# x of groups 4 and 5 transposed by DMA instead of by TensorE, between two sets of loads

## The chip, the cores and the metric

One core of one Trainium2 chip. The metric is the device time of one execution in microseconds (us). "Before" is the kernel as it was, "changed" the kernel with the change. A ratio is the mean time of one kernel's fast runs over that of the other's of the same rounds, so it is not quite the ratio of the medians quoted beside it.

## The reference

Attention within chunks of 64 tokens, then a feed-forward layer with a squared ReLU:

```python
scores = (1 / sqrt(64)) * q_c @ k_c^T          # chunks of 64 tokens, 8 x 8 heads, 576 tokens each
attn   = softmax(scores)
x      = (attn @ v_c)  rearranged to [4608, 512]
out    = (relu(x @ w_in) ** 2) @ w_out         # w_in 512 x 2048, w_out 2048 x 512
```

## The kernel before

The 4608 tokens are 18 groups of 256; two groups make a block of 512, for which the feed-forward layer runs (`ffn_in`, L360, then `ffn_out`, L412). While a block's matmuls run, the attention of the next block is slipped in between them: `plan` names for each slot (a few matmuls) what is issued there. A slot is a place in each engine's order, not a time. `TA` transposes q and k on TensorE; `C` and `TD` cast them on GpSimd and transpose them by DMA, from group 6 on; `SC` are the scores, `AV` the values, which leave x in SBUF; `XT` transposes x, as the feed-forward layer wants it with the features on the partitions.

```python
    FIRST_DMA_T = 6
    FIRST_DMA_X = 6
    # ... cut ...
    def transpose_x(g):
        # ... cut: xT tile of the block ...
        x = state.pop(("x", g))
        dst = xTs[j][:, c // 128:c // 128 + 2].rearrange("p t h q -> p (t h) q")
        if g >= FIRST_DMA_X:
            nc.sync.dma_start_transpose(out=dst, in_=x.rearrange("p t h a d -> p (t h a d)"))
            return
        ps = ps_att.tile([128, 1024], FP32, name="ps_att")
        psb = ps.bitcast(BF16)[:, 0:1024].rearrange("p (b q) -> p b q", q=128)
        for t in range(2):
            for hp in range(n_hp):
                nc.tensor.transpose(                                   # L342, 8 a group
                    out=psb[:, t * n_hp + hp, :],
                    in_=x[:, t, hp].rearrange("p a d -> p (a d)"), identity=ident)
        copy = nc.scalar.copy if g == 3 else nc.vector.tensor_copy
        copy(out=dst, in_=psb)                                         # L347
    # ... cut ...
        elif j == 1:       # block 1 (groups 2, 3): nxt = groups 4, 5; far = groups 6, 7
            loads = itertools.chain(*map(qk_pieces, far), v_pieces(far[0]))
            go_slots = range(14, 32)
            # ... cut ...
            for i, g in enumerate(nxt):
                for slot, f in ((21 + 4 * i, TA), (28 + 2 * i, SC), (33 + 2 * i, AV),
                                (38 + 3 * i, XT)):
                    at(slot, f, g)
            for i, g in enumerate(far):
                at(34 + 3 * i, C, g)
                at(36 + 3 * i, TD, g)
```

All loads and all DMA transposes are issued from SyncE, in order; output stores are issued from GpSimd (but for the last two).

The softmax here doesn't subtract the row's maximum and nothing guards it: scores larger than these inputs give would overflow.

## Time and profile before

| | us |
|---|---|
| median of the four executions beside the changed kernel | 294.42 |
| span in the profile | 292.4 |
| TensorE busy | 285.6 (98%) |

The prediction below shows what bounds the kernel; here are the rows that the change acts on, from the groups of instructions by line (last: busy us, mean ns of one, idle time before) and from the DMA issues (last: us from issue to landing).

```profile
L342 PE MATMUL ps_att<-ident,x 128*128 128x128 bf16 x32 | 2.6, 219 | 0.0
L347 DVE COPY xT<-ps_att 128x1024 bf16<-128x1024 bf16 x3 | 2.1, 692 | 4.4 <-PE ps_att L342 4.4
qkT<-qkb SPq DMA_TRANSPOSE x12, 5.8
xT<-x SPq DMA_TRANSPOSE x12, 3.3
```

32 transposes of L342 are those of groups 2 to 5, eight each. The 12 transposes of xT by DMA are those of groups 6 to 17. A busy time of 2.6 us for 32 instructions of 219 ns says that they overlap.

### The profile page before, as it was taken

Reading aid. Unit: us, or ns where it says so; the run is one execution under the profiler, and the core shown is the slowest. Engines: PE = TensorE matmul, PEld = TensorE weight load, DVE = VectorE, ACT = ScalarE, POOL = GpSimd, SP = SyncE. Lnnn points to the kernel's source line nnn. Section 1 sums busy time; section 2 is a strip of 40 time slices with the busy share of each in tenths; the row PEclk is TensorE's granted clock in tenths of the full one; section 3 lists DMA queues with packets and bytes.
Section 4 is the critical chain, followed back from the end, with each engine's and each line's share of the span. In section 5 each row is a group of like instructions: output and inputs, shape, how many; then the busy total and the mean of one; then the engine's idle time right before and its main releaser. Section 6 shows DMA issues by size and latency. Waiting matters only on the chain.

```text
span 292.4 us, 6471 instructions
## 1 busy us (share of the span) xinstructions
PE 285.6 (98%) x2661; PEld 141.7 (48%) x2661; DVE 111.0 (38%) x234; ACT 131.2 (45%) x214; POOL 66.8 (23%) x107
## 2 busy tenths in 40 slices
PE   7899999999999999999999999999999999999995
PEld 3454445885544444444444444444444444444444
DVE  0458413665414710571068105710472046104401
ACT  1557315775137513761376137612761276127410
POOL 2047824001510241042122113311043100230010
PEclk9999999999999999999999999999999999999999
DMA  7999999978999999999998899188999911331011
GB/s 233 248 349 366 352 294 255 345 160 192 214 165 209 211 213 206 250 198 232 263 232 170 189 231 214 37 184 211 201 209 224 202 39 36 74 72 36 0 74 72
DMA packets 145933, 56.00 MB, mean 191 GB/s; under 512 B 127024, under 2 KB 141616, under 8 KB 145904
## 3 DMA queue, kind: packets, MB, share of 16 engines
q1 hardware_dynamic: 142896, 46.28, 75.1%
q0 software_dynamic: 2864, 9.18, 10.2%
q8 instruction: 21, 0.34, 0.5%
q10 hardware_dynamic: 144, 0.13, 0.1%
q14 instruction: 8, 0.07, 0.1%
HBM read 36.70 MB, written 9.44 MB: 158 GB/s over the span
## 4 chain that ended last, share of the span: by engine, by line
PE 83%; DMA 8%; SPq 4%; POOL 2%; issue 0%; DVE 0%; DVEq 0%
PE ps_ffn L360 39%; PE ps_ffn L412 37%; DMA w_st<-in_moe_w_out_dram 4%; DMA w_st<-in_moe_w_in_dram 4%; PE ps_att L315 2%; SPq L138 2%; PE ps_att L291 2%; SPq L150 2%; PE ps_ffn L401 1%; PE ps_ffn L431 1%; PE ps_att L196 1%; POOL w_out_bf L179 1%; POOL w_in_bf L172 1%; PE ps_att L342 1%; POOL w_in_bf L168 1%
## 5 line engine op out<-in xcount | busy, mean ns | idle before, releaser
L360 PE MATMUL ps_ffn<-xT,w_in_bf 128*128 128x512 bf16 (+3 forms) x648 | 130.0, 356 | 0.2 <-POOL w_in_bf L168 0.2
L372 DVE TENSOR_TENSOR gT<-rl 128x512 bf16<-128x512 bf16 x144 | 71.2, 510 | 135.7 <-ACT rl L370 134.7
L412 PE MATMUL ps_ffn<-w_out_bf,gT 128*128 128x512 bf16 x496 | 109.3, 379 | 0.0
L370 ACT ACTIVATE rl<-ps_ffn 128x512 bf16<-128x512 f32 x144 | 85.1, 599 | 37.3 <-PE ps_ffn L360 35.8
L360 PEld LDWEIGHTS <-w_in_bf 128*128 128x128 bf16 x648 | 61.3, 98 | 60.4 <-POOL w_in_bf L168 0.9
L412 PEld LDWEIGHTS <-gT 128*128 128x128 bf16 x496 | 47.8, 98 | 56.3
L419 ACT COPY o_sb<-ps_ffn 128x512 f32<-128x512 f32 x31 | 18.2, 586 | 93.0 <-PE ps_ffn L412 93.0
L389 POOL DMA_DIRECT2D out_dram<-o_sb x39 | 21.2, 545 | 119.1 <-ACT o_sb L419 115.8
L270 POOL CAST qkb<-qk_sb 128x1024 bf16<-128x1024 f32 x24 | 25.8, 1085 | 76.2 <-DMA qk_sb<-in_q_dram 72.5
L323 DVE TENSOR_TENSOR x<-ps_att,rec 128x512 bf16<-128x512 f32 x36 | 24.9, 691 | 1.2
L298 ACT ACTIVATE e<-ps_att 128x1024 bf16<-128x1024 f32 x18 | 17.7, 1023 | 2.3 <-PE ps_att L291 2.3
L431 PE MATMUL ps_ffn<-w_out_bf,gT 128*128 128x512 bf16 x64 | 15.0, 379 | 0.3 <-POOL w_out_bf L179 0.3
L264 PE MATMUL ps_ffn<-zeros 128*128 128x512 bf16 x29 | 9.5, 466 | 1.3 <-POOL zeros L57 1.3
L179 POOL CAST w_out_bf<-w_st 128x1024 bf16<-128x1024 f32 x8 | 9.1, 1131 | 6.9 <-DMA w_st<-in_moe_w_out_dram 6.8
L315 PEld LDWEIGHTS <-e 64*64 64x64 bf16 x576 | 6.6, 107 | 7.5 <-DVE gT L372 2.1
L322 DVE RECIPROCAL rec<-ps_att 128x8 f32<-128x8 f32 x36 | 7.2, 199 | 7.1 <-PE ps_att L315 7.0
L431 PEld LDWEIGHTS <-gT 128*128 128x128 bf16 x64 | 6.0, 98 | 7.4 <-issue 0.6
L315 PE MATMUL ps_att<-ve_sb,e 64*64 64x65 bf16 x288 | 8.8, 196 | 0.1
L315 PE MATMUL ps_att<-vo_sb,e 64*64 64x65 bf16 x288 | 8.8, 196 | 0.0
L205 ACT COPY qkT<-ps_att 128x512 bf16<-128x512 bf16 x8 | 4.3, 589 | 9.7 <-PE ps_att L196 9.7
L172 POOL CAST w_in_bf<-w_st 128x1024 bf16<-128x1024 f32 x7 | 7.4, 1062 | 2.9 <-DMA w_st<-in_moe_w_in_dram 2.9
L291 PEld LDWEIGHTS <-qkT 64*64 64x64 bf16 x576 | 5.7, 108 | 4.7 <-issue 3.4
(33 smaller groups left out, 59.8 us busy)
## 6 DMA issues: line engine op xcount, KB each, us to landing
out_dram<-o_sb POOLq DMA_DIRECT2D x31, 256.0 KB, 4.0
qk_sb<-in_q_dram SPq DMA_DIRECT2D x20, 256.0 KB, 5.3
qk_sb<-in_k_dram SPq DMA_DIRECT2D x20, 256.0 KB, 5.4
ve_sb<-in_v_dram SPq DMA_DIRECT2D x32, 128.0 KB, 4.1
w_st<-in_moe_w_in_dram SPq DMA_DIRECT2D x8, 512.0 KB, 6.7
w_st<-in_moe_w_out_dram SPq DMA_DIRECT2D x8, 512.0 KB, 6.1
vo_sb<-in_v_dram SPq DMA_DIRECT2D x24, 128.0 KB, 3.6
qk_sb<-in_q_dram SPq DMA_DIRECT2D x4, 512.0 KB, 7.0
```

The source lines that it names most:

```text
L179: nc.gpsimd.tensor_copy(out=w_out_bf[:, 2 * i:2 * i + 2, :], in_=st)
L270: nc.gpsimd.tensor_copy(out=qkb[:, which], in_=qk[g][which].rearrange("p t h d -> p (t h d)"))
L298: nc.scalar.activation(out=e.rearrange("p a h t q -> p (a h t q)"), in_=ps, func=AF.Exp, scale=scale)
L315: nc.tensor.matmul(out=ps[64 * p:64 * p + 64, a, hp * (D + 1):(hp + 1) * (D + 1)], lhsT=e[64 * c:64 * c + 64, a, hp, t, :], rhs=vb[64 * c: ...
L323: nc.vector.tensor_tensor(out=x[:, t].rearrange("p h a d -> p a h d"), in0=o[:, :, :, 0:D], in1=rec.to_broadcast([128, 2, n_hp, D]), op=AL ...
L360: nc.tensor.matmul(out=h[:, o:o + n], lhsT=w_in_bf[:, dt, ft * 128:(ft + 1) * 128], rhs=xT[:, c // 128:(c + n) // 128, dt, :], start=(dt = ...
L370: nc.scalar.activation(out=rl, in_=h, func=AF.Relu)
L372: nc.vector.tensor_tensor(out=gTs[j][:, ft:ft + per, c:c + 512 // per], in0=r3, in1=r3, op=ALU.mult)
L389: eng.dma_start(out=out[b * S + s:b * S + s + m, cols], in_=o_sb[p:p + m, :])
L412: nc.tensor.matmul(out=o_ps, lhsT=gT[:, ft, tt * 128:(tt + 1) * 128], rhs=w_out_bf[:, ft, :], start=(ft == 0), stop=(ft == n_ft - 1))
L419: nc.scalar.copy(out=o_sb, in_=o_ps)
L431: nc.tensor.matmul(out=o_ps[tt], lhsT=gT[:, ft, tt * 128:(tt + 1) * 128], rhs=w_out_bf[:, ft, :], start=(ft == 0), stop=(ft == n_ft - 1))
```

## The change

Groups 4 and 5 go by DMA too. For that their `XT` moves up in the order, and the value loads of group 6 and the q,k transposes of groups 6 and 7 move behind it. As built, the change removes 16 transposes and their 16 weight loads from TensorE and two copies from VectorE, and puts two DMA transposes into SyncE's order, ahead of the value loads of group 6. Nothing else moves on any engine.

```diff
-    FIRST_DMA_X = 6
+    FIRST_DMA_X = 4
@@ block 1
-            go_slots = range(14, 32)
+            go_slots = [*range(14, 22), *range(39, 44)]
-                                (38 + 3 * i, XT)):
+                                (36 + 2 * i, XT)):
-                at(36 + 3 * i, TD, g)
+                at(44 + 2 * i, TD, g)
```

## The prediction

> **What bounds the kernel now.** I read the page first: busy time per engine, the slices, and the chain that ended last.
>
> ```profile
> PE 285.6 (98%) x2661; PEld 141.7 (48%) x2661; DVE 111.0 (38%) x234; ACT 131.2 (45%) x214; POOL 66.8 (23%) x107
> PE   7899999999999999999999999999999999999995
> PEclk9999999999999999999999999999999999999999
> DMA  7999999978999999999998899188999911331011
> PE 83%; DMA 8%; SPq 4%; POOL 2%; issue 0%; DVE 0%; DVEq 0%
> ```
>
> TensorE is busy in every slice at its full granted clock, and 83% of the chain is TensorE. The DMA engines are nearly full from slice 10 (73 us) to slice 20. Then I took the chain in order of time, because the mean share does not tell which wait ends last in the stage that changes:
>
> ```profile
> 72.96 0.39 PE ps_att L315 x32
> 73.35 2.70 PE ps_ffn L412 x12
> 76.04 0.45 PE ps_att L342 x8
> 76.49 2.59 PE ps_ffn L412 x12
> 79.08 0.45 PE ps_att L342 x8
> 79.53 5.18 PE ps_ffn L412 x24
> 84.71 7.77 PE ps_ffn L360 x36
> ...
> 95.55 0.38 PE ps_att L291 x32
> ```
>
> From 44.9 us to 289 us this chain is TensorE without a gap. So here a TensorE instruction removed is time removed, unless some input comes later than TensorE then wants it. The two pieces of L342 (eight transposes each, x of groups 4 and 5) are what the change takes away. L360 at 84.71 is the first user of their result, L291 at 95.55 the scores of group 7.
>
> **What the Trainium skill says.** (1) "Perfetto Trace Analysis", Identifying the Most-Contended Engine: busy share of matmuls is no good measure of the distance to the limit. The trace agrees (98% beside 48% of weight loads), so I cost the change from the chain, not from the 98%. (2) "TensorE: Matmul & The Clock Gate", Part 4: PE-mode transpose: a 128x128 bf16 transpose measured some 390 ns alone and 275 ns in a kernel, and its output in PSUM needs a copy. Here one shows 219 ns, but eight together hold the chain only 0.45 us, because they are pipelined; I use 0.45. (3) "DMA: Bandwidth & Descriptors", Issuing engines are not separate DMA queues: transfers share 16 engines whoever starts them. The trace agrees, as the landing times below show. (4) Same page, Latency and other measured facts: transposing DMA at 261 GB/s in one kernel. This trace has a duration: late in the kernel, one x transpose has the engines to itself.
>
> ```profile
> 246.00:248.00 2.00, 2.00 (x41) 0.94 (x40) 1.25 (x4) 1.19 (x2) 0.00 (x0) 1.00 0.49 95
> 248.00:250.00 2.00, 2.00 (x11) 0.94 (x10) 1.72 (x5) 0.00 (x0) 0.00 (x0) 1.00 0.19 36
> ```
>
> The last two columns are DMA share and GB/s: 2 x 0.49 + 2 x 0.19 = 1.36 us of all 16 engines for 262 KB, 193 GB/s, slower than that figure. The measurement decides.
>
> **The change part by part.**
>
> Removed from TensorE: 16 transposes, two pieces of 0.45 us, all on the chain: **-0.90 us**. Nothing else moves on TensorE: in the order of its instructions as built, the 32 rows (16 weight loads, 16 transposes) are the only difference.
>
> Removed from VectorE: two copies from PSUM of 0.69 us. VectorE is 38% busy, and none of its work stands in this stretch of the chain: 0 us.
>
> Added to the DMA: two transposes of x. The built order of the SyncE queue shows them as the only addition, ahead of the five value loads of group 6. The new slots of the qkT transposes (44 and 46) and of the loads change no order beyond that. When do they start? The queue now:
>
> ```profile
> 71.61 2.39 SPq L131 DMA_DIRECT2D qk_sb<-in_q_dram  x1
> 74.05 0.78 SPq L131 DMA_DIRECT2D qk_sb<-in_k_dram  x1
> 74.87 1.64 SPq L138 DMA_DIRECT2D ve_sb<-in_v_dram  x2
> 76.56 2.00 SPq L150 DMA_DIRECT2D vo_sb<-in_v_dram  x3
> 78.74 7.62 SPq L277 DMA_TRANSPOSE qkT<-qkb  x2
> 86.40 1.22 SPq L138 DMA_DIRECT2D ve_sb<-in_v_dram  x2
> ```
>
> The x transposes take the place at 74.87. The last multiplication that makes x of group 4 ends at 72.84 and that of group 5 at 75.06 (timeline of VectorE), so SyncE hardly waits. One issue took 1.26 us (median of the 12 there are): 74.9 and 76.1. The value loads issued at those times landed in 4.5 and 4.0 us, transposes of x in 3.0 to 5.4, so xT is there by about 81.5; L360 wants it at 84.7 - 0.9 = 83.8. **Hidden, with some 2 us to spare.**
>
> What it pushes: everything after on the queue starts about 2 x 1.26 = 2.5 us later, and the engines get 2 x 1.36 = 2.7 us more work. The shares in two-us windows are 0.63 at 74 to 76, then 1.07 to 1.53 up to 86 (packets overlap, so more than 1 is possible), so little of it fits in a hole: at most 2 x (1 - 0.63) = 0.7 us. Estimate of the push: **2.0 to 2.7 us**. Who feels it? Landing now, the time when TensorE now uses it, and what is left after 0.9 us earlier use and 2.7 us later landing (the worst of my estimate):
>
> - qkT of group 7: issued 81.9, landing 10.3 us later, 92.2; scores at 95.5: 3.3 left now, **-0.3** after (+0.4 with a push of 2.0).
> - qkT of group 6: issued 78.7, +8.2, 86.9; scores at 92.4: 5.5 now, 1.9 after.
> - values of group 7: last issued 88.6, +5.7, 94.3; used at 101.0: 6.7 now, 3.1 after.
> - xT of group 7: issued 105.4, +4.3, 109.7; used at 114.5: 4.8 now, 1.2 after.
> - qkT of group 9: issued 111.5, +7.5, 119.0; used at 123.4: 4.4 now, 0.8 after.
>
> So one deadline is about met or just missed. That row's landing view (the window holds this transpose alone):
>
> ```profile
> L277 SPq DMA_TRANSPOSE qkT<-qkb x1: 4457/4457/4457, 81.9 to 81.9; - x1
> DMA to landing us min/median/max: 10.3/10.3/10.3
> ```
>
> Those 10.3 us are queueing: the least that such a transpose took in this trace is 4.5. Two output stores, issued at 82.2 and 85.6, lie on the same engines and take 8.9 and 6.3 us.
>
> Sum: -0.90 us on the chain, plus a wait of 0 to about 1 us before the scores of group 7. I put it at +0.25 us on average (four chances in ten of about 0.6 us): 294.34 - 0.90 + 0.25 = 293.7.
>
> **Rivals.** *A. The whole gain arrives (293.4).* For it: every other transfer has slack, and qkT of group 7 now meets less of the stores, which come 0.4 to 0.9 us earlier while it comes later. Against: its slack is gone by arithmetic. *B. A new wait takes the gain back (294.0 to 296).* The pushed qkT of group 7 comes 0.5 to 2.5 us late, or, if the push isn't absorbed, qkT of group 9 too. For it: DMA shares above 1 and landings of 8 to 10 us between 79 and 92. Against: an early wait gives the DMA queue time and loosens the later deadlines, so the waits don't add up without end; SyncE stands idle from 180 to 187.7 anyway, so nothing lasts beyond. *C. xT itself late.* It would stop L360 at 83.8 at once. For it: the first transpose follows eight loads of 262 KB. Against: 2 us of slack, and the loads there land in 4 to 4.5 us. *D. The transposes were hidden anyway (294.3).* It would need something other than TensorE to end the waits at 76 and 79; the chain shows no gap there, so I give it little.
>
> **Range and chances.** The centre is 293.6, between A's 293.4 and the sum 293.7. Low end: 293.4 less the scatter of the three runs (0.3) is about 292.9. High end: B with two waits of about 0.8 us, 293.4 + 1.6, about 295.1. 2% is 5.9 us: more than six times all that the removed work costs, and for slower it would take a push more than twice that of my estimate at several deadlines. So within 2% is nearly certain.
>
> **What would show each step.** L342 with 16 transposes instead of 32 and two transposes more by DMA of xT; no L342 between 73 and 84 in the chain, and L360 starting at about 83.8 (right) or later with a wait for the DMA of xT (C). Landing of qkT of group 7 near 94.5, and the weight load of its scores near 94.6: a wait on that DMA there is B, none is A. The last TensorE work starting 0.9 us earlier than now is A. I am wrong if the time goes outside the range: if the push is well over 2.7 us because mixed transposes and stores slow each other more than now, or if a wait shows at three or more of the five deadlines.

## The result, and the profile after

| | before | changed |
|---|---|---|
| median, us | 294.42 (294.0 to 294.53) | 293.34 (293.18 to 294.32) |
| ratio of fast runs | | 0.9973 (95%: 0.9949 to 0.9997) |
| span in the profile | 292.4 | 291.6 |

The same rows of the changed kernel:

```profile
L342 PE MATMUL ps_att<-ident,x 128*128 128x128 bf16 x16 | 1.4, 220 | 0.0
L347 DVE COPY xT<-ps_att 128x1024 bf16<-128x1024 bf16 x1 | 0.7, 691 | 0.6 <-PE ps_att L342 0.6
xT<-x SPq DMA_TRANSPOSE x14, 3.9
qkT<-qkb SPq DMA_TRANSPOSE x12, 6.9
```

Half of L342 is gone, and two of the copies of L347. The chain in order of time (start us, us, what), in the stage that changed:

```profile
73.10 0.39 PE ps_att L315 x30
73.49 0.16 issue
73.65 10.31 PE ps_ffn L412 x47
83.96 7.77 PE ps_ffn L360 x36
91.73 0.38 PE ps_att L291 x32
```

Where two pieces of 0.45 us stood in the chain before, there is one run of L412 now, and L360 follows it without a wait for the DMA. (47 where it should be 48: some matmul records are missing from a trace.)

One measure serves for the rest of this text: **the stretch**, from the first weight load of the scores of group 5 to that of the scores of group 6. It holds both XT. These are the weight loads, before and after (start us, us, what; in brackets the idle time of the weight loads before it):

```profile
68.01 0.33 PEld L291 LDWEIGHTS <-qkT 64*64 64x64 bf16 x32 [0.21 <-issue]
92.41 0.34 PEld L291 LDWEIGHTS <-qkT 64*64 64x64 bf16 x32 [0.42 <-issue]
...
68.16 0.33 PEld L291 LDWEIGHTS <-qkT 64*64 64x64 bf16 x32 [0.21 <-issue]
91.66 0.33 PEld L291 LDWEIGHTS <-qkT 64*64 64x64 bf16 x32 [0.42 <-issue]
94.73 0.34 PEld L291 LDWEIGHTS <-qkT 64*64 64x64 bf16 x32 [0.42 <-issue]
```

The stretch was 68.01 to 92.41 = 24.40 us before, and is 68.16 to 91.66 = 23.50 us now: 0.90 us less. It doesn't feel what happens before 68 us, where executions differ by some tenths.

Now the SyncE queue of the changed kernel (start us, us, what):

```profile
70.67 3.03 SPq L131 DMA_DIRECT2D qk_sb<-in_k_dram  x1
74.22 3.37 SPq L336 DMA_TRANSPOSE xT<-x  x2
77.64 1.14 SPq L138 DMA_DIRECT2D ve_sb<-in_v_dram  x2
78.83 1.97 SPq L150 DMA_DIRECT2D vo_sb<-in_v_dram  x3
80.98 9.27 SPq L277 DMA_TRANSPOSE qkT<-qkb  x2
90.29 1.13 SPq L138 DMA_DIRECT2D ve_sb<-in_v_dram  x2
```

The pair of x is issued from 74.22, the second at 75.7, and lands 3.9 us later, at 79.7: four us ahead of L360. The qkT transposes start 2.2 us later than before (80.98 against 78.74), the value loads behind them 3.9 us later (90.29 against 86.40). That was to make qkT of group 7 late. Its landing view, for this one transpose:

```profile
L277 SPq DMA_TRANSPOSE qkT<-qkb x1: 6076/6076/6076, 84.2 to 84.2; - x1
DMA to landing us min/median/max: 9.5/9.5/9.5
```

It landed at 93.7, the weight load of its scores came at 94.73: one us to spare. No wait. Nor was any of the prediction's other four deadlines missed: qkT of group 6 landed at 91.0 for a weight load at 91.7, the values of group 7 at 95.5 for 100.2, x of group 7 at 111.3 for 113.4, qkT of group 9 at 120.6 for 122.5.

### The profile page after: what moved, and what is told of

The parts are those of the page before. It is cut to its first block, busy times and chain, and to the rows that moved or that the text cites. A ratio compares the mean times of both kernels' runs of the same rounds, so it can differ in the third digit from the quotient of the medians.

```text
span 291.6 us, 6425 instructions
## 1 busy us (share of the span) xinstructions
PE 282.5 (97%) x2624; PEld 140.5 (48%) x2645; DVE 109.1 (37%) x232; ACT 131.2 (45%) x214; POOL 66.3 (23%) x107
## 4 chain that ended last, share of the span: by engine, by line
PE 81%; DMA 8%; SPq 4%; POOL 2%; DVE 1%; ACT 1%; issue 1%; DVEq 0%
PE ps_ffn L360 37%; PE ps_ffn L412 37%; DMA w_st<-in_moe_w_out_dram 4%; DMA w_st<-in_moe_w_in_dram 4%; SPq L138 2%; PE ps_att L315 2%; SPq L150 2%; PE ps_att L291 2%; PE ps_ffn L401 1%; PE ps_ffn L431 1%; PE ps_att L196 1%; POOL w_out_bf L179 1%; POOL w_in_bf L172 1%; ACT rl L370 1%; POOL w_in_bf L168 1%
## 5 line engine op out<-in xcount | busy, mean ns | idle before, releaser
L360 PE MATMUL ps_ffn<-xT,w_in_bf 128*128 128x512 bf16 (+3 forms) x648 | 130.0, 356 | 0.0
L412 PE MATMUL ps_ffn<-w_out_bf,gT 128*128 128x512 bf16 x481 | 107.8, 379 | 0.9 <-issue 0.2
L360 PEld LDWEIGHTS <-w_in_bf 128*128 128x128 bf16 x648 | 61.0, 98 | 60.0 <-POOL w_in_bf L172 0.5
L412 PEld LDWEIGHTS <-gT 128*128 128x128 bf16 x496 | 47.8, 98 | 56.9
L270 POOL CAST qkb<-qk_sb 128x1024 bf16<-128x1024 f32 x24 | 25.6, 1084 | 85.2 <-DMA qk_sb<-in_q_dram 84.4
L431 PE MATMUL ps_ffn<-w_out_bf,gT 128*128 128x512 bf16 x61 | 14.5, 379 | 1.1 <-POOL w_out_bf L179 0.7
L264 PE MATMUL ps_ffn<-zeros 128*128 128x512 bf16 x26 | 8.8, 457 | 1.4 <-POOL zeros L57 1.3
L431 PEld LDWEIGHTS <-gT 128*128 128x128 bf16 x64 | 6.0, 98 | 7.9 <-issue 1.0
```

The costliest lines, as they stand in the source:

```text
L270: nc.gpsimd.tensor_copy(out=qkb[:, which], in_=qk[g][which].rearrange("p t h d -> p (t h d)"))
L360: nc.tensor.matmul(out=h[:, o:o + n], lhsT=w_in_bf[:, dt, ft * 128:(ft + 1) * 128], rhs=xT[:, c // 128:(c + n) // 128, dt, :], start=(dt = ...
L412: nc.tensor.matmul(out=o_ps, lhsT=gT[:, ft, tt * 128:(tt + 1) * 128], rhs=w_out_bf[:, ft, :], start=(ft == 0), stop=(ft == n_ft - 1))
L431: nc.tensor.matmul(out=o_ps[tt], lhsT=gT[:, ft, tt * 128:(tt + 1) * 128], rhs=w_out_bf[:, ft, :], start=(ft == 0), stop=(ft == n_ft - 1))
```

## The experiments

Eleven kernels ran on the chip. All but one gave the right result. The table has what they measured; the stretch is that of the one profiled execution (in the last three rows the order of the work differs, so it would not compare), "before" the median of the kernel before on the same chip.

| run | median us | before | ratio (95%) | stretch us |
|---|---|---|---|---|
| changed, first time | 293.34 | 294.42 | 0.9973 (0.9949 to 0.9997) | 23.50 |
| again | 294.00 | 294.82 | 0.9980 (0.9946 to 1.0014) | 23.50 |
| again2 | 293.58 | 294.45 | 0.9976 (0.9964 to 0.9988) | 23.50 |
| no_transpose | 293.92 | 294.82 | 0.9970 (0.9947 to 0.9993) | 23.51 |
| slots_only | 294.83 | 294.51 | 1.0009 (0.9994 to 1.0024) | 24.53 |
| old_slots | 301.53 | 294.82 | 1.0249 (1.0219 to 1.0280) | 29.61 |
| extra1 | 293.74 | 294.82 | 0.9965 (0.9939 to 0.9990) | 23.50 |
| extra2 | 295.71 | 294.51 | 1.0057 (1.0018 to 1.0096) | 26.05 |
| extra3 | 299.10 | 294.51 | 1.0163 (1.0132 to 1.0195) | 27.20 |
| t5 | 295.02 | 294.51 | 1.0025 (1.0005 to 1.0044) | |
| t5b | 293.01 | 294.45 | 0.9995 (0.9947 to 1.0043) | |
| t5c | 293.88 | 294.42 | 0.9971 (0.9931 to 1.0012) | |

### The changed kernel twice more

No edit.

> The changed kernel once more, in five rounds, since its gain (0.3%) is near the scatter. Theory A (the removed 0.90 us of TensorE work arrives whole, nothing waits): 0.7 to 1.1 us faster than the kernel before, chain without a wait at the scores of groups 6 and 7. Rival B (in some executions the qkT transposes of groups 6 and 7 land after TensorE wants them; they had 0.6 and 1.0 us to spare in the first profile): runs scatter by about a us above the fastest, and the mean gain is 0.3 to 0.7 us.

> The changed kernel a third time, on the same chip as the further step: 0.7 to 1.1 us below the kernel before, and the stretch from the scores of group 5 to those of group 6 again 23.5 us, wherever the qkT transposes of groups 6 and 7 land.

The stretch is 23.50 us in all three profiles, to the hundredth. The times agree with a gain of 0.6 to 0.8 us (the ratios 0.9973, 0.9980 and 0.9976 of 294.5 us), though the interval of the second includes no gain. What differs is the landing of qkT of group 7. In the second profile:

```profile
L277 SPq DMA_TRANSPOSE qkT<-qkb x1: 2297/2297/2297, 83.4 to 83.4; - x1
DMA to landing us min/median/max: 5.6/5.6/5.6
```

5.6 us, where the same program had taken 9.5. Counted from the start of the stretch, so that executions can be compared, qkT of groups 6 and 7 landed at these times (TensorE wants them at 23.5 and 26.6 in the changed kernel):

| profile | group 6 | group 7 |
|---|---|---|
| before | 18.96 | 24.16 |
| changed, first | 22.89 | 25.55 |
| again | 18.75 | 20.23 |
| again2 | 19.02 | 21.44 |
| extra1 | 22.85 | 24.59 |
| extra2 | 26.01 | 28.02 |
| extra3 | 27.16 | 29.32 |

In two of three profiles of the changed kernel both landed earlier than, or as early as, in the one profile before, with more work on the DMA. So a landing read from one profile was no fixed number here: the same transfer of the same program differs by 5.3 us. What makes the difference is open. The DMA engines moved 152, 155 and 69 GB/s in the two-us windows from 84 to 90 us of the first profile, and 287, 134 and 325 in those of the second, at busy shares of 1.29 to 1.51 and of 1.88, 0.61 and 1.19; and two output stores that GpSimd issued meanwhile took 9.4 and 8.5 us in the first, 5.4 and 4.2 us in the second. So the stores were slow too, not the transposes alone; why is not shown.

As for rival B, one execution of "again" took 296.76 us where the others took 293.06 to 294.15. It alone brings the mean gain down to 0.6 us, which lies in rival B's range. An execution of the kernel before took 296.33 in the same rounds, so the time alone proves nothing. But the mean granted clock of the slow one (the share of its full clock that TensorE got) is 0.994; the other 14 executions of the changed kernel, and all of the kernel before, have 0.998 to 1.000. Below, 0.994 is the clock of the profiled executions in which TensorE waited 2.5 us or more and then ran at half clock. So a long wait in one execution of 15 is likely; no profile shows whether it was for qkT, and rival B stays open to that extent.

### No transpose of x of groups 4 and 5 at all

```diff
+        if g in (4, 5):
+            nc.vector.tensor_copy(out=dst.rearrange("p b q -> p (b q)"),
+                                  in_=x.rearrange("p t h a d -> p (t h a d)"))
+            return
```

Its output is wrong, which doesn't matter for the time.

> The changed kernel without any transpose of x of groups 4 and 5: VectorE copies x untransposed into xT (wrong result on purpose). Theory A (the two DMA transposes are hidden wholly): same time as the changed kernel within 0.3 us, 0.9 us faster than before; the qkT transpose of group 7 lands about 1.5 us earlier than in the changed kernel (near 92), and TensorE does not use that. Rival B (the DMA transposes cost something on the way): 0.5 us or more faster than the changed kernel.

The stretch is 23.51 us, as with the two DMA transposes, and the median of 293.92 is that of the changed kernel in the same rounds (294.00). **In these profiles the two DMA transposes cost nothing on TensorE's path.** Two copies by VectorE stand in for them and cost nothing either, so the copies that the change removes account for no gain. The push is there all the same: counted from the start of the stretch, the first qkT transpose is issued at 9.8 us without them, and at 12.8, 12.0 and 12.0 in the three profiles with them. (The second qkT transpose is issued at 81.4, but the record of its landing is missing from this trace, so the expected landing near 92 can't be checked.)

### The slots alone

The diff of the change, with FIRST_DMA_X left at 6.

> The new slots alone, x of groups 4 and 5 still transposed on TensorE. Theory (the gain is the removed TensorE work and nothing else): the stretch from the scores of group 5 to those of group 6 is 24.4 us as in the kernel before, time the same as before within 0.5 us. Rival (part of the gain came from the slots): stretch below 24.2.

24.53 us: 0.13 more than before. Time as before. Its chain holds L342 for 0.58 and 0.45 us, which are the 0.13 us. So the slots give nothing, and with "no_transpose" the removed TensorE work is left as the gain.

### The DMA alone, in the old slots

Against the kernel before:

```diff
-    FIRST_DMA_X = 6
+    FIRST_DMA_X = 4
```

> Only the switch to DMA for groups 4 and 5, with the slots of the kernel before: the two transposes of x then stand behind the value loads of group 6 and between and behind the qkT transposes of groups 6 and 7 in the SyncE queue. Theory (the place in the queue decides): the second transpose of x is issued at about 88 us and lands at 92 to 95, L360 wants it at 83.8, so TensorE waits 8 to 11 us once, and the time is 300 to 304 us, 2 to 3% slower than before. Rival (16 engines have room, the place doesn't matter): 293.4, as the changed kernel.

The same transposes in another place of SyncE's order: 301.5 us, 2.5% slower than before. The chain says why:

```profile
81.60 2.53 SPq L277
...
84.22 4.56 DMA xT<-x
88.78 0.14 issue
88.92 9.26 PE ps_ffn L360 x36
98.17 0.38 PE ps_att L291 x32
```

xT of group 5 is issued behind the qkT transpose of group 7 and lands at 88.8; TensorE stands 4.5 us (the chain of waits names this DMA). It came earlier than I expected (issue at 84.2, not 88), so the wait was half of what I expected. But look at the fourth line: the same 36 matmuls that took 7.77 us take 9.26. After the wait, TensorE ran at half clock for a while:

```profile
88.80:90.00 1.20, 1.08 (x3) 0.43 (x4) 0.00 (x0) 0.00 (x0) 0.00 (x0) 0.50 0.97 213
90.00:92.00 2.00, 2.00 (x7) 0.72 (x6) 0.43 (x1) 0.60 (x1) 0.00 (x0) 0.59 1.05 208
92.00:94.00 2.00, 2.00 (x11) 0.94 (x10) 0.77 (x2) 1.30 (x3) 0.00 (x0) 1.00 1.20 220
```

The third column from the right is the granted clock. 4.5 us of wait and 1.5 us of slow matmuls are 6.0 of the 6.1 us by which this stretch exceeds 23.50. That the time fell into the expected range was luck: half of the wait, and a clock that I had not thought of. The profile is of the fastest of the five executions; the others have mean clocks of 0.983 to 0.989 against its 0.994, so more time at half clock, which no profile shows. The Trainium skill, "TensorE: Matmul & The Clock Gate", section Why this matters for your kernels, says to leave no TensorE idle gap of more than some 3 us between matmul bursts, since the clock then falls back to half. With its gap of 4.5 us this trace agrees.

### More transposes in the same place

Two, four and six transposes of x of group 5 more, into a scratch tile, right behind the two:

```diff
             nc.sync.dma_start_transpose(out=dst, in_=x.rearrange("p t h a d -> p (t h a d)"))
+            if g == 5:
+                for _ in range(2):          # extra2: 4, extra3: 6; bufs too
+                    junk = att_pool.tile([128, 8, 128], BF16, name="junk", bufs=2)
+                    nc.sync.dma_start_transpose(out=junk, in_=x.rearrange("p t h a d -> p (t h a d)"))
             return
```

> The changed kernel with two more transposes of x of group 5 right behind the two, into a scratch tile: the suspected cost doubled. Theory (the queue push is hidden only up to the slack left at the qkT transposes of groups 6 and 7, 0.6 and 1.0 us): they land 1.5 to 2.7 us later, TensorE waits for them 0.5 to 2 us, time 0.5 to 2 us above the changed kernel, with the wait before the weight load of the scores of group 6 or 7. Rival (the DMA has room to spare): no change from the changed kernel, within 0.3 us.

My expectation failed. With the added work doubled the stretch is 23.50 us and the time that of the changed kernel. qkT of group 7 was issued at 88.2, four us later than in the changed kernel's first profile, and landed 4.4 us after, at 92.6, sooner than there (the last of block 1's stores had landed at 90.6). The slack of 0.6 and 1.0 us that I had read from one profile was not the slack that the kernel has. But little room was left in this profile: 0.65 us at qkT of group 6, and behind the stretch x of group 7 landed at 113.31, so that the weight loads of L360 waited 0.3 us for it (the wait list names this DMA). The matmuls did not start later for that: 22.0 us after the scores of group 6, as in the changed kernel.

> Four more transposes of x of group 5 behind the two of the change. With two more the time did not move: the qkT transposes of groups 6 and 7 then landed 22.9 and 24.6 us after the scores of group 5 and TensorE wanted them at 23.5 and 26.6. Theory (there is a push, it was within the slack): about 3 us more push, so the qkT transpose of group 6 lands at 25 to 27, the stretch from the scores of group 5 to those of group 6 grows from 23.5 to 25 to 27 us, time 1.5 to 4 us above the changed kernel. Rival (the push is made up elsewhere on the DMA engines, there is no limit near): the stretch stays 23.5, time as the changed kernel.

> Six more transposes of x. Theory: 3 us more than with four: stretch 28 to 31 us, time 4 to 8 us above the changed kernel. Rival: stretch 23.5, time as the changed kernel.

With four more, the limit is passed, as expected. The weight loads of extra2 (its edit moves line numbers, L360 is L365 here):

```profile
89.96 1.39 PEld L365 LDWEIGHTS <-w_in_bf 128*128 128x128 bf16 x7
94.33 0.34 PEld L291 LDWEIGHTS <-qkT 64*64 64x64 bf16 x32 [2.98 <-DMA qkT<-qkb]
94.71 0.55 PEld L365 LDWEIGHTS <-w_in_bf 128*128 128x128 bf16 x4
95.52 0.15 PEld L365 LDWEIGHTS <-w_in_bf 128*128 128x128 bf16 x1 [0.26 <-issue]
...
```

In brackets stands the idle time and what ended it: 2.98 us for qkT, at the scores of group 6. Of these, 0.42 us stand there without a wait too; the gap between the matmuls was 2.5 us, by which the stretch grew. And it is followed by weight loads that come singly, 0.43 us apart: the twelve matmuls between the scores of groups 6 and 7 took 4.38 us instead of 2.70. The window from 96 to 98 us shows a granted clock of 0.50. This profile is of the slowest of four executions, 298.69 us; the other three took 295.01 to 295.99 at a clock of 1.000, so they too were slower than the changed kernel, but without the slow matmuls. With six more the wait is 4.13 us (3.6 between the matmuls) and the stretch 27.20 (I had expected 28 to 31), the time 299.1, in the expected range. So the push that the prediction feared exists; in these profiles **two transposes fit in this place, four just fit, six don't** (counting the two of the change).

### One step further

If removed TensorE work is gained whole, q and k of group 5 could go by DMA as well: 32 transposes, 1.0 us of the chain.

```diff
-    FIRST_DMA_T = 6
+    FIRST_DMA_T = 5
@@ block 0: loads
+            loads = itertools.chain(*map(qk_pieces, far), v_pieces(far[0]))
@@ block 1
-            loads = itertools.chain(*map(qk_pieces, far), v_pieces(far[0]))
-            go_slots = [*range(14, 22), *range(39, 44)]
+            loads = itertools.chain(v_pieces(nxt[1]), *map(qk_pieces, far), v_pieces(far[0]))
+            go_slots = [*range(10, 22), *range(39, 44)]
+            at(4, C, nxt[1])
+            at(9, TD, nxt[1])
```

(Cut: TA for group 4 only, scores of group 5 at slot 32, and scores and values of groups 6 and 7 one or two slots later.)

> The same idea one step further: besides x of groups 4 and 5, also q and k of group 5 are transposed by DMA (cast on GpSimd), its transpose put ahead of the value loads of group 5, scores and values of groups 5, 6, 7 some slots later. It takes 32 transposes (1.0 us of the chain) off TensorE. Theory (removed TensorE work on this chain is gained whole as long as each transfer lands before use): 292.4, 0.9 to 1.1 us below the changed kernel, about 1.9 below the kernel before. Rival (the qkT transpose of group 5 lands after its use near 68, or the push makes those of groups 6 and 7 late): a wait of 1 us or more there and no gain over the changed kernel.

No gain: the rival's number, but not its waits. There was none at qkT of groups 5, 6 or 7. TensorE's weight loads waited 1.33 us for xT of group 5, which landed at 83.5 behind the last loads of q and k of group 7, and 1.78 us at the scores of group 7, which I had put right behind the values of group 6 although both want the two attention buffers in PSUM. Between the matmuls these gaps were 0.9 and 1.7 us, and after both the granted clock stayed at 1.00.

The second form (against the first) issues the transposes of x ahead of the last two of those loads, and moves the scores of group 7 two slots:

```diff
-            go_slots = [*range(10, 22), *range(39, 44)]
+            go_slots = [*range(10, 20), 39, 40, *range(42, 47)]
-                at(34 + 3 * i, C, g)
-                at(44 + 2 * i, TD, g)
+                at(34 + 7 * i, C, g)
+                at(41 + 6 * i, TD, g)
```

(Cut: the slots of SC, AV and XT of groups 6 and 7.)

> The further step mended. Its first form lost what it gained in two waits: TensorE waited 1.3 us for xT of group 5 (landed 83.5, behind the last loads of q and k of group 7) and 1.8 us for a PSUM buffer at the scores of group 7 (put right behind the values of group 6). Now the transposes of x stand ahead of the last two loads of q and k of group 7, and the scores of group 7 come two slots later. Theory (removed TensorE work is gained whole if nothing lands late): stretch from the scores of group 4 to the next block's first scores without a wait over 0.5 us, 292.4, about 1 us below the changed kernel and 0.6 to 0.7% below the kernel before. Rival (the DMA has no room left for a third transpose in this stretch): another wait of 1 us or more, no gain over the changed kernel.

Both waits are gone, but a new one of 0.92 us came, at 112.8, for xT of group 7. Four of six executions took 292.4 to 293.1 us, two took 296.4 and 296.7. The median is below that of both kernels, but the ratio of the means, 0.9995, is not clear of 1.

The third form (against the second) moves the value loads of group 8 behind the transposes of x of groups 6 and 7:

```diff
-                go_slots = [*range(14), 17, 18, *range(22, 32)]
+                go_slots = [*range(12), *range(22, 32)]
```

(Cut: scores, values and XT of groups 8 and 9 one slot later.)

> The further step, mended again. In five of its executions it took 292.4 to 293.1 us but in two 296.5, and its profile shows the transpose of x of group 7 landing 0.1 us before TensorE goes on, after a wait of 0.9 us, and the qkT transpose of group 9 landing with 0.4 us to spare. Now x of groups 6 and 7 is transposed ahead of the value loads of group 8, and scores and values of groups 8 and 9 come one slot later. Theory (the late landings made both the wait and the scatter): no wait over 0.5 us on TensorE after 45 us, 292 us or a little below, all executions within 1.5 us. Rival (the slow executions have another cause): the scatter stays, some executions at 296.

(The text miscounts: it was four and two of six.) Now three executions took 292.5 to 292.7, the others 295.1 to 296.1. The profile fell on a slow one: its scores of group 3 come at 54.9 us, where the others have 52.7 to 53.5, behind a gap of 1.97 us at L431, in the stage in which the weights of w_out arrive; and it waits 1.02 us for qkT of group 5. So the late landing of xT was mended (no wait there), but the scatter stayed: of the 2.7 us by which this profile's span exceeds that of t5b, 2.1 stand before 55 us, away from what I moved last. Whether the other slow executions lost their time in the same place no profile shows, and why is open. No version is shown to beat the changed kernel.

## Why the prediction was right

The time of 293.34 us lies in the range of 292.9 to 295.1, 0.26 below the 293.6 predicted. That closeness is partly luck: the interval of the ratio, 0.9949 to 0.9997, allows a gain of 0.1 to 1.5 us, so the times can't tell rival A's 293.4 from the sum's 293.7. The chains can. By its steps:

- *The removed work, -0.90 us, all on the chain:* right. The stretch is shorter by 0.90 us in three profiles of three, and "slots_only" and "no_transpose" show that nothing else gave it. The sign that the prediction named, the last TensorE work (L401) starting 0.9 us earlier, is less clear: 284.82 against 285.49, and counted from the scores of group 5 it comes 0.82, 0.89 and 0.57 us earlier in the three profiles.
- *The VectorE copies, 0 us:* they are gone; the gain is accounted for without them, and "no_transpose" has it with two copies in their place.
- *xT hidden with some 2 us to spare:* right, and on the safe side: it landed at 79.7, not 81.5, so the spare was four us. The issue started at 74.2, not 74.9. L360 started at 83.96 (83.8 predicted).
- *The push of 2.0 to 2.7 us:* right for the issue of the first qkT transpose (2.2 us later than in the profile before; 2.2 to 3.0 against "no_transpose"). Carried over to the landings, it failed: qkT of group 7 landed 1.4 us later in one profile and 3.9 and 2.7 us earlier in the two others, counted from the start of the stretch. The step took each landing from one profile as a fixed number and added the push to it. That the 10.3 us were "queueing" was its reading, which no run tests.
- *The average wait of +0.25 us before the scores of group 7:* this term of the sum was too large. It measured 0 in three profiles, and 0 even with the push doubled; one slow execution of 15 may have had such a wait. It was also more than its own table gives: 0.6 us in four cases of ten, where the worst of the estimate was 0.3 us late.
- *Rival A* is what happened. *Rival B*, the wait, is real, but only with three times the transposes that the change adds were all executions slower. *Rival C* is what "old_slots" shows: the same transposes would have cost 2.5% without the new slots. *Rival D* fell.
- *The low end of the range* does not follow from its terms: 293.4 less 0.3 is 293.1, not 292.9. The result lies above both.

I had no step for the clock: in three profiles here a gap of 2.5 us or more between matmuls cost another 1.5 to 1.7 us. It didn't matter in the profiles of the changed kernel, where no such gap came, but the high end of the range was built without it.

## What to carry to other kernels

Where one engine fills the chain without a gap and every input still comes in time, work taken off it is gained whole, and only as much as its pieces in the chain say (0.45 us for eight pipelined transposes, not eight times 219 ns). Work moved to a DMA queue that serves everything is paid for by its place in the order: ask what stands behind it, when each of those is wanted, and how much room there is, and test the room by adding work rather than reading it from one landing. Here a gap of 2.5 us or more between matmuls (2.5, 3.6 and 4.5) was followed by matmuls at half clock and cost more than its length; gaps of 1.7 us and less were not.

## What the Trainium skill lacked or had wrong

- "TensorE: Matmul & The Clock Gate", Part 4: PE-mode transpose: 390 ns alone and some 275 ns in a kernel for a 128x128 bf16 transpose. Here one shows 219 ns, and eight in a row hold the chain for 0.45 us, 56 ns each; that section has no figure for transposes in a row.
- The same page, Why this matters for your kernels: idle gaps of more than some 3 us halve the clock. Here a shorter one did: 2.5 us between the matmuls (2.98 between the weight loads; the stretch grew by 2.55) in "extra2", with a granted clock of 0.50 from 96 to 98 us; gaps of 1.7 us and less did not. The price was 1.5 to 1.7 us on top of the wait (12 matmuls took 4.38 us instead of 2.70, 36 took 9.26 instead of 7.77).
- "DMA: Bandwidth & Descriptors", Latency and other measured facts: 261 GB/s for a transposing DMA in one kernel. Here a transpose of x of 262 KB, alone on the engines, took 1.36 us of all of them: 193 GB/s.
- I found no page that says how much the landing of the same transfer varies between executions of one program: here qkT of group 7 landed 20.2, 21.4 and 25.6 us after the same instruction.
